# Turning three normalized chunks through VectorE and memory in place of TensorE transposes

## The chip, the cores and the metric

The kernel runs on one core of one Trainium2 chip. The metric is the device time of one execution in microseconds (us), the median of three runs. TensorE (PE in the profile) does the matrix products, VectorE (DVE) and ScalarE (ACT) read and write the accumulators in PSUM, GpSimd (POOL) works on SBUF alone, and SyncE (SP) issues nearly all transfers. Each engine takes its instructions strictly in the order in which the program wrote them.

## The reference

Four layers follow one another: attention A, feed-forward B, attention A, feed-forward B, each added to its input. There are 2048 rows of 448 values, 16 heads of 28, one key and value head shared by all, and a feed-forward of width 1792.

```python
q = (x @ wq) per head;  k = x @ wk;  v = x @ wv
p = softmax(q k^T * 28**-0.5);   A(x) = (p v) @ wo
B(x) = (silu(x @ w_gate) * (x @ w_up)) @ w_down
x = x + A(layernorm(x)); x = x + B(layernorm(x)); x = x + A(layernorm(x)); x = x + B(layernorm(x))
```

All of it is float32. The kernel keeps that precision by splitting each operand into a high part, rounded to the matrix format, and a low part, the rest; a product is then three matmuls: high by high, high by low, low by high.

## The kernel before, in words

The 2048 rows are handled as four chunks of 512 rows (chunk c is rows 512c to 512c+511), each chunk as four tiles of 128 rows on the 128 partitions. `xres` holds the running sum in SBUF.

Before a layer multiplies, a chunk is normalized (`norm_steps`, lines 210 to 233: statistics on VectorE, the scale on GpSimd, the normalized tile `xn` by VectorE with 64 columns copied by GpSimd) and turned, so that features lie on partitions. `flip` (lines 241 to 262) does the turning with TensorE: four 128x128 transposes make one 128x512 PSUM bank, `flipped` then has the bank copied, rounded, into `xh`, and the rest, bank minus `xh`, put into `xl` by VectorE. There are four such banks to a chunk. 448 features are three and a half times 128, so in the fourth bank the upper 64 partitions hold the rest of the same features, with `xd` as a copy of their high part.

Attention (`scores`, lines 530 to 692) runs 16 iterations i, four heads of one chunk each, of 16 steps kt. In a step TensorE makes 128x2048 scores, ScalarE takes their exponential in two instructions (lines 573, 574) and TensorE multiplies two steps later by the values (line 604). At step 10 of iterations 4, 8 and 12 `between_steps` puts in the output product of the chunk that is done (line 551). Around it `post` collects a finished iteration's sums: small transfers `rs`, `rd`, `rb`, and one product and one split on GpSimd (lines 615 to 643). For the iteration after next, four transfers fetch `qraw` at step 4, GpSimd splits it at step 7 and a transfer adds the `rows` at step 9.

Feed-forward needs the chunks turned again. In the kernel before

- chunk 0 is normalized in iteration 5 and flipped in the output-product slots of iterations 8 and 12, two banks in each, through the single bank `one`;
- chunk 1 is normalized in iteration 13 and flipped at the head of `FeedForward.rest` (line 863), after the last output product;
- chunks 2 and 3 are normalized in `rest` and soon after, and flipped in the middle of the units that go before their first use (line 870, `mid`).

Feed-forward's work is units: `unit(gi, c, n)` (line 791) multiplies chunk c with one block of 128 features of gate and up in two halves (lines 801 to 814), with down-products of the unit before between and behind them. The two first units, of chunk 0, run inside `scores`, ahead of the last chunk's output product; the next in program order are the two of chunk 1, the two of chunk 2, the two of chunk 3. In every half the matmuls run through the four 128-row blocks of the turned chunk in order, the last of the half needing the upper rows of the fourth block. `accumulate` (line 731) adds a finished group to `xres`: two of four tiles through a `stage` buffer and GpSimd (line 743). The buffers of the turned chunks 1 to 3 (`xb`) lie in the memory that the attention's own buffers (`wp`) leave at its end.

A second version of the whole program (`full`) stands in a branch at the end that the profiled execution does not take.

The order on every engine is the order in which the code calls the instructions; nothing reorders it.

Of the kernel before, what the change touches and what calls it, by code (L numbers as in the profile page):

```python
# [8 lines left out]
F32 = mybir.dt.float32  # L9
# [6 lines left out]
P = 128  # L16
# [38 lines left out]
def forward(  # L55
# [154 lines left out]
    def norm_steps(c, pool=pers):  # L210

        got = {}
        cs = slice(4 * c, 4 * c + 4)

        def stat(t):
            nc.vector.bn_stats(stats[:, 4 * c + t, :], xres[:, 4 * c + t, :])
            nc.vector.bn_aggr(mv[:, 4 * c + t, :], stats[:, 4 * c + t, :])

        def scale():
            rstd = pers.tile([P, 4], F32, name="rstd", bufs=2)  # L220
            nc.gpsimd.tensor_scalar(rstd, mv[:, cs, 1], 1.0, EPS, ALU.mult, ALU.add)
            nc.gpsimd.tensor_tensor(rstd, rstd, halfn, ALU.pow)
            got["r"] = rstd

        def apply(t):
            if t == 0:
                got["x"] = pool.tile([P, 4, 512], F32, name="xn")
            o, i, r = got["x"][:, t, 0:D], xres[:, 4 * c + t, :], got["r"][:, t : t + 1]
            nc.vector.tensor_scalar(o, i, mv[:, 4 * c + t, 0:1], r, ALU.subtract, ALU.mult)  # L229
            nc.gpsimd.tensor_copy(got["x"][:, t, D:512], o[:, 384:D])  # L230

        fs = [lambda t=t: stat(t) for t in range(4)] + [scale]
        return fs + [lambda t=t: apply(t) for t in range(4)], got
# [7 lines left out]
    def flip(got, tiles, ks=range(4), place=None):  # L241

        for k in ks:
            pt = place if place is not None else bank(wide[-1])[1]
            for t in range(4):
                nc.tensor.transpose(pt[:, P * t : P * t + P], got["x"][:, t, P * k : P * k + P], ident)  # L246
            flipped(tiles, k, pt, nc.vector.tensor_copy if place is not None else nc.scalar.copy)

    def flipped(tiles, k, pt, copy):
        xh, xl, xd = tiles  # L250
        if k < 3:
            copy(xh[:, k, :], pt)
            nc.vector.tensor_tensor(xl[:, k, :], pt, xh[:, k, :], ALU.subtract)  # L253
            return
        if xd is None:
            copy(xh[:, k, :], pt)
            high = xh[64:128, k, :]
        else:
            copy(xh[0:64, k, :], pt[0:64, :])
            copy(xd[64:128, :], pt[64:128, :])  # L260
            high = xd[64:128, :]
        nc.vector.tensor_tensor(xh[64:128, k, :], pt[64:128, :], high, ALU.subtract)

    def product_T(po, a_h, a_l, tiles):

# [37 lines left out]
    class Attention:  # L303
# [226 lines left out]
        def scores(self, ff):  # L530
            next(switch)
            with tc.tile_pool(name=f"at{self.layer}", bufs=1) as wp:
# [44 lines left out]
                def between_steps(n):  # L577

                    i, kt = divmod(n, NT)
                    free, one = threes[(n + 1) % 2], banks[7]  # L580
                    if full:
                        self.lent = free[:, 0, :]
                        self.advance(KC)
                        if kt == 11 and i + 1 < len(GR):
                            self.places[i + 1](free[:, 1, :])
                    if not todo or kt != 10:
                        return
                    c = todo.pop()
                    ks = list({8: (0, 1), 12: (2, 3)}.get(i, ()))
                    adds = []  # L590
                    for t in (1, 2, 3):
                        adds.append(outproj(c, t, free[:, t - 1, :]))
                        if ks:
                            flip(got, X0, [ks.pop(0)], one)
                    for f in adds:
                        f()
                    outproj(c, 0, one)()
# [45 lines left out]
                    return rest  # L643

                X0 = xtile(xpool)
                fs, got = norm_steps(0)
                fs1, got1 = norm_steps(1)
                ff.norms[1] = got1
                ff.second = norm_steps(2)
                last = NT * len(GR)  # L650
                for n in range(last):
                    i, kt = divmod(n, NT)
                    if kt == 4 and 2 < i + 2 < len(GR):
                        self.stack(i + 2)
                    if kt == 7 and 2 < i + 2 < len(GR):
                        self.parts(i + 2)
                    if kt == 9 and 2 < i + 2 < len(GR) and not full:
                        self.rows(i + 2)
                    if i in (2, 3) and kt == 8:
                        load_wo(i - 2)  # L660
                    if n == NT and ff.nxt:
                        ff.nxt.below(nc.sync)
                    if kt == 8 and 10 < i <= 11 + FG:
                        ff.W[i - 11] = weights(i - 11)
                    step(n)
                    if not full:
                        between_steps(n)
                    if n > 1:
                        pv(n - 2)
                    if full:  # L670
                        between_steps(n)
                    if n in due:
                        due.pop(n)()
                    if i in (5, 13, 14) and kt > 5:
                        for f in {5: fs, 13: fs1, 14: ff.second[0][:5]}[i][kt - 6 : kt - 5]:
                            f()
                for n in (last - 2, last - 1):
                    pv(n)
                self.lent = None
# [16 lines left out]
    class FeedForward:  # L696
        def __init__(self, layer):
            self.layer, self.X, self.W, self.norms = layer, {}, {}, {}
            self.pend, self.soon, self.dn, self.flip, self.mid, self.left = [], [], {}, 0, {}, []
            self.nxt = Attention(1) if layer == 0 else None  # L700

        def down(self, fs, fc, d, hh, hl):

# [53 lines left out]
        def hand_over(self, c):  # L757

            a = self.nxt
            fs, got = norm_steps(c)  # L760
            for f in fs[:5]:
                f()
            a.pool = self.stage
            a.X[c] = xtile(xpool if c == 0 else self.xbp)

            def ready():
                for f in fs[5:]:
                    f()
                if c > 1:
                    a.norms[c] = got  # L770

            if c == NC - 1:
                a.plan[8, 0] = [ready]
                return
            self.soon.append([1, ready])
            if c < 2:
                self.mid[len(groups) - 1, c + 2, 0] = [lambda ks=ks: flip(got, a.X[c], ks) for ks in ((0, 1), (2, 3))]
                self.soon.append([2, lambda: [a.project() for _ in range(2 - c)]])

        def turned(self, c, ks=range(4)):  # L780
            if c not in self.X:
# [74 lines left out]
        def rest(self, xb):  # L856
            self.stage = xb.enter_context(tc.tile_pool(name=f"stage{self.layer}", bufs=2))
            self.xbp = xb.enter_context(tc.tile_pool(name=f"xb{self.layer + 1}", bufs=3))
            xd = xb.enter_context(tc.tile_pool(name=f"xd{self.layer}", bufs=1))
            self.xd = [xd.tile([P, 512], F32R, name=f"xd{c}") for c in range(NC)]  # L860
            dma(self.xd[0][64:128, :], self.X[0][0][0:64, 3, :])
            self.X[0] = (*self.X[0][:2], self.xd[0])
            self.turned(1)
            fs2, self.norms[2] = self.second
            fs3, self.norms[3] = norm_steps(3)
            for f in fs2[5:] + fs3[:5]:
                f()
            self.soon.append([1, lambda: [f() for f in fs3[5:]]])
            for c in (2, 3):
                self.mid[0, c - 1, 1] = [lambda c=c, ks=ks: self.turned(c, ks) for ks in ((0, 1), (2, 3))]  # L870
            for gi, fs in enumerate(groups):
                if self.layer == 1 and fine is not None and gi in (2, 3):
                    self.verdict(gi == 3)
                    if gi == 3:
                        tc.mark_branch_hint_location("again", engines=(ET.Activation, ET.DVE, ET.Pool, ET.SP, ET.PE))
                for c in range(NC):
                    for n in range(len(fs)):
                        if gi or c:
                            self.unit(gi, c, n)
# [90 lines left out]
```

## Time and profile before

| what | us |
|---|---|
| median of three runs | 2043.53 (2042.91 to 2044.38) |
| span of the profiled execution | 2041.5 |
| what lies outside the span, median less span | 2.0 |
| PE busy / ACT busy / POOL busy / DVE busy in it | 2018.5 / 1311.0 / 536.7 / 460.0 |
| attention scores, first and second | about 75 to 596 and 1083 to 1604 |
| feed-forward, first and second | about 596 to 1000 and 1604 to 2041 |

The page gives no separate time for the profiled execution but its span; the 2.0 us between it and the median are taken as what lies around the span. A row of a timeline gives start and duration in us, engine, source line, operation, the tile written and the tiles read, the count of instructions merged in the row, and in brackets how long the engine sat idle before it and what ended that. A row of windows gives, for a stretch, each engine's busy time and count, the granted clock of TensorE (PEclk, 1.00 is full), the share of the transfer engines and GB/s.

### The profile page before, as it was taken

What the parts mean: (1) busy time and instruction counts of PE and PEld (TensorE: products, weight loads), DVE (VectorE), ACT (ScalarE), POOL (GpSimd) and SP (SyncE); (2) the same over time, 40 slices, a digit from 0 to 9 for tenths busy, and PEclk for the clock granted to TensorE, in tenths of its full rate; (3) what the DMA queues carried; (4) which work ended last, traced back from release to release, by engine and by line L of the source; (5) the groups of instructions that cost most, each with busy time, mean ns of one, the idle gap of its engine ahead of it and who ended that gap; (6) DMA issues with size and microseconds to landing.
All of it is one profiled execution on the core that took longest, in us unless ns stands there. A gap on an engine that the chain in (4) does not pass through costs nothing.

```text
span 2041.5 us, 43675 instructions
## 1 busy us (share of the span) xinstructions
PE 2018.5 (99%) x18627; PEld 1275.7 (62%) x18627; DVE 460.0 (23%) x890; ACT 1311.0 (64%) x2152; POOL 536.7 (26%) x601
## 2 busy tenths in 40 slices
PE   8999999999999999999999999999999999999998
PEld 7533434334348999999883334343343689988887
DVE  6300101001104323222451001010011242232322
ACT  3699898997973333333348998979979533333332
POOL 4313121021302333333341221111222122333320
PEclk9999999999999999999999999999999999999999
DMA  4201000011100111100031110100110000111102
GB/s 146 66 22 28 21 12 22 12 37 27 32 12 19 31 31 31 31 16 26 21 93 34 30 30 12 22 12 22 27 45 13 25 17 20 31 31 31 31 1 74
DMA packets 76512, 63.44 MB, mean 31 GB/s; under 512 B 22904, under 2 KB 63224, under 8 KB 76312
## 3 DMA queue, kind: packets, MB, share of 16 engines
q1 hardware_dynamic: 74580, 58.93, 10.4%
q8 instruction: 147, 2.41, 0.5%
q10 hardware_dynamic: 1732, 1.66, 0.3%
q14 instruction: 53, 0.43, 0.1%
HBM read 47.72 MB, written 12.32 MB: 29 GB/s over the span
## 4 chain that ended last, share of the span: by engine, by line
PE 50%; ACT 46%; DVE 1%; issue 1%; DMA 1%; POOL 0%; ACTq 0%; SPq 0%; DVEq 0%; POOLq 0%
PE bank L292 39%; ACT pt L574 31%; ACT pt L573 15%; PE bank L272 4%; PE three L551 2%; PE bank L551 2%; PE bank L246 1%; PE bank L604 1%; DMA wr<-in_A_wk_dram 1%; PE three L567 0%; DVE xl L253 0%; DMA kt<-stage 0%; DVE xn L229 0%; PE bank L398 0%; DVE vt L505 0%
## 5 line engine op out<-in xcount | busy, mean ns | idle before, releaser
L574 ACT ACTIVATE pt<-three 128x1536 f32<-128x1536 f32 x512 | 741.2, 1448 | 0.0
L604 PE MATMUL bank<-pt,vsb 128*32 128x512 f32 x4096 | 547.0, 606 | 0.5 <-ACT pt L574 0.5
L567 PEld LDWEIGHTS three<-qstack,keys 32*128 32x128 f32 x4608 | 252.9, 183 | 449.7 <-ACT pt L573 393.2
L567 PE MATMUL three<-qstack,keys 32*128 32x512 f32 x4608 | 498.5, 426 | 2.3 <-DVE vt L505 1.1
L567 PE MATMUL bank<-qstack,keys 32*128 32x512 f32 x1536 | 493.5, 426 | 2.9 <-ACT pt L573 2.9
L292 PE MATMUL bank<-xh,wgh 64*128 64x512 f32 x1728 | 447.6, 390 | 0.4
L292 PE MATMUL bank<-xh,wgl 64*128 64x512 f32 x1404 | 368.2, 390 | 0.0
L573 ACT ACTIVATE pt<-bank 128x512 f32<-128x512 f32 x512 | 305.8, 597 | 74.3 <-PE bank L567 68.1
L292 PE MATMUL bank<-xl,wgh 64*128 64x512 f32 x1296 | 335.1, 390 | 0.0
L292 PE MATMUL bank<-wdh,h 64*128 64x448 f32 x1792 | 331.2, 364 | 1.2 <-ACT h L827 0.8
L292 PEld LDWEIGHTS bank<-xh,wgh 64*128 64x128 f32 x1728 | 262.9, 184 | 19.1 <-DVE xl L253 1.5
L743 POOL TENSOR_TENSOR xres<-stage,xres 128x448 f32<-128x448 f32 x108 | 127.4, 1199 | 497.9 <-ACT stage L742 497.9
L638 POOL TENSOR_TENSOR o<-o 128x512 f32<-128x512 f32 x32 | 41.1, 1285 | 821.5 <-DMA o<-rd 748.5
L292 PEld LDWEIGHTS bank<-wdh,h 64*128 64x128 f32 x1792 | 242.5, 184 | 15.2 <-issue 2.7
L567 PEld LDWEIGHTS bank<-qstack,keys 32*128 32x128 f32 x1536 | 244.3, 183 | 4.5 <-ACT pt L573 4.3
L299 ACT COPY seen<-bank 128x1 f32<-128x1 f32 x664 | 81.7, 163 | 247.3 <-PE bank L292 244.4
L292 PEld LDWEIGHTS bank<-xh,wgl 64*128 64x128 f32 x1404 | 216.6, 184 | 13.8
L292 PE MATMUL bank<-wdl,h 64*128 64x448 f32 x896 | 217.7, 366 | 0.0
L825 ACT ACTIVATE sg<-bank 128x512 f32<-128x512 f32 x112 | 67.3, 601 | 220.0 <-PE bank L292 214.9
L292 PEld LDWEIGHTS bank<-xl,wgh 64*128 64x128 f32 x1296 | 196.3, 184 | 10.5
L604 PEld LDWEIGHTS bank<-pt,vsb 128*32 128x32 f32 x4096 | 80.9, 108 | 190.0 <-issue 175.2
L826 DVE TENSOR_TENSOR sg<-bank,sg 128x512 f32<-128x512 f32 x112 | 77.4, 691 | 500.0 <-ACT sg L825 491.1
(115 smaller groups left out, 1736.6 us busy)
## 6 DMA issues: line engine op xcount, KB each, us to landing
o<-rd SPq DMA_DIRECT2D x32, 256.0 KB
qd<-stage SPq DMA_DIRECT2D x32, 224.0 KB
qraw<-qd SPq DMA_DIRECT2D x128, 56.0 KB
wdr<-in_B_w_down_dram SPq DMA_DIRECT2D x28, 224.0 KB
wr<-in_B_w_gate_dram SPq DMA_DIRECT2D x28, 192.0 KB
wr<-in_B_w_up_dram SPq DMA_DIRECT2D x28, 192.0 KB
out_dram<-xres SPq DMA_DIRECT2D x15, 224.0 KB
wrk<-kt SPq DMA_DIRECT2D x8, 256.0 KB
```

Source lines behind the costliest of these rows:

```text
L272: nc.tensor.matmul(po, a, b, start=(i == 0), stop=(i == len(seq) - 1))
L292: nc.tensor.matmul(po, a, b, start=start, stop=stop, skip_group_check=True)
L299: nc.scalar.copy(seen[:, i : i + 1], po[:, 0:1])
L551: nc.tensor.matmul(po[:, 0:D], a[:, g, ts_], b[:, g, :], start=(g + z == 0), stop=(g == NG - 1 and z == 2))
L567: nc.tensor.matmul(three[:, j, :] if j < 3 else one, k[js, kp, ks], q[js, part, :], start=(z == 0), stop=(z == 2), tile_position=(32 * j, 0),)
L573: nc.scalar.activation(pt1, one, AF.Exp, scale=SCALE)
L574: nc.scalar.activation(pt, three, AF.Exp, scale=SCALE)
L604: nc.tensor.matmul(accs[i][32 * j : 32 * j + 32, :], vsb[:, kt, :], pts[n][j], start=(kt == 0), stop=(kt == NT - 1), skip_group_check=True,)
L638: nc.gpsimd.tensor_tensor(rb, oraw, rb, ALU.mult)
L743: nc.gpsimd.tensor_tensor(r, s, r, ALU.add)
L825: nc.scalar.activation(sg, pg[0], AF.Silu)
L826: nc.vector.tensor_tensor(sg, pg[1], sg, ALU.mult)
```

## The change

Chunks 0, 1 and 2 ahead of each feed-forward are no longer turned by TensorE. In attention's iterations 5, 9 and 13 a chunk is normalized, one call at each of steps 6 to 14. At the next four steps (step 15 and steps 0 to 2 of the following iteration) `turn_tile` has VectorE transpose a 128x512 tile in blocks of 32x32 into a new buffer `tb`, and SP issues four transfers that carry the blocks, in pieces of 128 bytes, to their places in a 512x512 tensor in memory, which then holds the turned chunk: 16 transfers to a chunk.

Chunk 0 is read back in iteration 7 by one 1 MB transfer and split by GpSimd (`halved`) at its steps 5, 8, 11 and 14. Chunk 1 is read back into `xn` in iteration 15, and `rest` begins with its split by GpSimd (`parts`): for each of three blocks a rounding copy and a subtraction, for the fourth two 64-partition copies and a subtraction, nine operations. Then SP reads chunk 2 into the same `xn` (`fetch(2)`), and GpSimd splits it likewise. Chunk 3 is flipped by TensorE as before.

```diff
+    def turn_tile(got, tb, raw, t):
+        nc.vector.transpose(tb[:, t, :], got["x"][:, t, :])
+        to = raw.rearrange("(b d) (t g w) -> t g d b w", d=32, g=4, w=32)
+        for g in range(4):
+            nc.sync.dma_start(to[t, g], tb[32 * g : 32 * g + 32, t, :].rearrange("d (b w) -> d b w", w=32))
+
+    def halved(tiles, r, ks=range(4)):
+        xh, xl, xd = tiles
+        for k in ks:
+            if k < 3:
+                split(xh[:, k, :], xl[:, k, :], r[:, k, :])
+        if 3 not in ks:
+            return
+        if xd is None:
+            nc.gpsimd.tensor_copy(xh[:, 3, :], r[:, 3, :])
+            high = xh[64:128, 3, :]
+        else:
+            nc.gpsimd.tensor_copy(xh[0:64, 3, :], r[0:64, 3, :])
+            nc.gpsimd.tensor_copy(xd[64:128, :], r[64:128, 3, :])
+            high = xd[64:128, :]
+        nc.gpsimd.tensor_tensor(xh[64:128, 3, :], r[64:128, 3, :], high, ALU.subtract)
...
-                        if ks:
-                            flip(got, X0, [ks.pop(0)], one)
...
+                for c in range(NC - 1):
+                    fs, got = norm_steps(c)
+                    ff.raw[c] = dram.tile([512, 512], F32, name=f"xt{self.layer}_{c}")
+                    fs += turns(c, got)
+                    for n, f in enumerate(fs):
+                        aside[16 * (4 * c + 5) + 6 + n] = f
+                for n, f in enumerate(back()):
+                    aside[16 * 7 + 2 + 3 * n] = f
+                aside[16 * 15 + 2] = lambda: ff.fetch(1)
...
+        def fetch(self, c):
+            self.got[c] = pers.tile([P, 4, 512], F32, name="xn")
+            nc.sync.dma_start(self.got[c], self.raw[c].rearrange("(k p) n -> p k n", p=P))
+
+        def parts(self, c):
+            self.X[c] = xtile(self.xbp, self.xd[c])
+            halved(self.X[c], self.got.pop(c))
...
-            self.turned(1)
-            fs2, self.norms[2] = self.second
+            self.parts(1)
+            self.fetch(2)
+            self.parts(2)
             fs3, self.norms[3] = norm_steps(3)
-            for f in fs2[5:] + fs3[:5]:
+            for f in fs3[:5]:
                 f()
             self.soon.append([1, lambda: [f() for f in fs3[5:]]])
-            for c in (2, 3):
-                self.mid[0, c - 1, 1] = [lambda c=c, ks=ks: self.turned(c, ks) for ks in ((0, 1), (2, 3))]
+            self.mid[0, 2, 1] = [lambda ks=ks: self.turned(3, ks) for ks in ((0, 1), (2, 3))]
```

More of the change, by code (lines that the diff above doesn't have):

```diff
@@ L588, in between_steps @@
                     c = todo.pop()
-                    ks = list({8: (0, 1), 12: (2, 3)}.get(i, ()))
                     adds = []
@@ L645, in scores, with turns, one, back @@
                 X0 = xtile(xpool)
[L646 to L649, printed above, removed]
+                def turns(c, got):
+                    at_ = {}
+                    def one(t):
+                        if t == 0:
+                            at_["tb"] = wp.tile([P, 4, 512], F32, name="tb")
+                        turn_tile(got, at_["tb"], ff.raw[c], t)
+                    return [lambda t=t: one(t) for t in range(4)]
+                def back():
+                    at_ = {}
+                    def load():
+                        at_["r"] = wp.tile([P, 4, 512], F32, name="tb")
+                        nc.sync.dma_start(at_["r"], ff.raw[0].rearrange("(k p) n -> p k n", p=P))
+                    return [load] + [lambda k=k: halved(X0, at_["r"], [k]) for k in range(4)]
+                aside = {}
+                for c in range(NC - 1):
[7 more added lines that the diff above has]
+                aside[16 * 15 + 2] = lambda: ff.fetch(1)
                 last = NT * len(GR)
@@ L673, in scores @@
                         due.pop(n)()
-                    if i in (5, 13, 14) and kt > 5:
-                        for f in {5: fs, 13: fs1, 14: ff.second[0][:5]}[i][kt - 6 : kt - 5]:
-                            f()
+                    if n in aside:
+                        aside[n]()
                 for n in (last - 2, last - 1):
@@ L700, in __init__ @@
             self.nxt = Attention(1) if layer == 0 else None
+            self.raw, self.got = {}, {}
         def down(self, fs, fc, d, hh, hl):
```

## The prediction

> **What bounds the kernel now.** I read the page first: the busy line, the granted clock and the chain that ended last.
>
> ```profile
> PE 2018.5 (99%) x18627; PEld 1275.7 (62%) x18627; DVE 460.0 (23%) x890; ACT 1311.0 (64%) x2152; POOL 536.7 (26%) x601
> PEclk9999999999999999999999999999999999999999
> PE 50%; ACT 46%; DVE 1%; issue 1%; DMA 1%; POOL 0%; ACTq 0%; SPq 0%; DVEq 0%; POOLq 0%
> ```
>
> Half the chain is PE (feed-forward, projections, output products) and half ACT (the exponentials of attention); DVE, POOL and the transfers carry nearly none. So what DVE and SP are given is free as long as nobody waits for it, and the question is where PE or ACT waits for turned chunks. There are three such places, the same in both layers: the output-product slots of iterations 8 and 12, the head of feed-forward (chunk 1), and the middle of its second unit pair (chunk 2).
>
> Slots: the timeline of ACT at step 10 of iterations 4, 8 and 12 in layer 1 (the idle time stands in the bracket), two rows of plain steps for the step length, and the row of the list of waits that groups them.
>
> ```profile
> 228.85 0.60 ACT L573 ACTIVATE pt<-bank 128x512 f32<-128x512 f32 x1 [10.16 <-PE bank L567]
> 230.80 0.60 ACT L573 ACTIVATE pt<-bank 128x512 f32<-128x512 f32 x1
> 232.69 0.60 ACT L573 ACTIVATE pt<-bank 128x512 f32<-128x512 f32 x1
> ...
> 361.48 0.60 ACT L573 ACTIVATE pt<-bank 128x512 f32<-128x512 f32 x1 [11.04 <-PE bank L567]
> ...
> 494.46 0.60 ACT L573 ACTIVATE pt<-bank 128x512 f32<-128x512 f32 x1 [11.33 <-PE bank L567]
> ACT pt L573 <- PE bank L567: 68.1, 10, 11.3
> ```
>
> Iteration 4 has no flips, 8 and 12 have two banks each: they cost 0.88 and 1.17 us. The list has 68.1 us in ten waits, and twice (10.16 + 11.04 + 11.33) is 65.1, so layer 2 pays the same.
>
> Head of feed-forward: the chain between 615 and 665 us, and one row of the PE timeline there.
>
> ```profile
> 616.59 2.62 PE bank L551 x12
> 619.21 0.45 PE bank L246 x4
> ...
> 621.65 10.08 PE bank L292 x83
> 631.72 1.03 PE bank L246 x8
> ...
> 634.18 1.02 PE bank L246 x8
> 624.07 0.36 PE L292 MATMUL bank<-wdh,h 64*128 64x448 f32 x1
> ```
>
> The last output product ends at 619.21, chunk 1 is flipped, and the first half of its first unit is through at 624.07, where the first down-product starts. Chunk 2's flips sit at 631.72 and 634.18. What they really take shows in the spacing of ACT's silu, one to a unit:
>
> ```profile
> 628.01 0.60 ACT L825 ACTIVATE sg<-bank 128x512 f32<-128x512 f32 x1 [1.96 <-PE bank L292]
> 637.75 0.60 ACT L825 ACTIVATE sg<-bank 128x512 f32<-128x512 f32 x1 [1.29 <-PE bank L292]
> 645.49 0.60 ACT L825 ACTIVATE sg<-bank 128x512 f32<-128x512 f32 x1 [1.96 <-PE bank L292]
> 662.98 0.60 ACT L825 ACTIVATE sg<-bank 128x512 f32<-128x512 f32 x1 [1.96 <-PE bank L292]
> 670.28 0.60 ACT L825 ACTIVATE sg<-bank 128x512 f32<-128x512 f32 x1 [2.14 <-PE bank L292]
> ```
>
> A plain unit is 7.30 us (662.98 to 670.28). The unit with chunk 2's flips takes 9.74, the one after it 7.74: together 2.9 us over.
>
> **The change, part by part.** All sums are per layer, against the profiled execution (span 2041.5 us); the median of the runs shown is 2.0 us above that, and I carry the 2.0 as constant.
>
> 1. Slots of iterations 8 and 12: without flips they should take what iteration 4's takes: 0.88 + 1.17 = -2.05 us.
>
> 2. DVE's transposes and the transfers in attention. The nearest rows, of the groups by shape, of SP's timeline twice, and the rate line of the transfer view of 14 to 19 us, when those two large reads ran:
>
> ```profile
> L400 DVE STREAM_TRANSPOSE sg<-bank 128x512 f32<-128x512 f32 x8 | 5.7, 717 | 22.0 <-PE bank L398 21.9
> 110.11 2.50 SPq L620 DMA_DIRECT2D rs<-o  x4
> 11.58 2.87 SPq L887 DMA_DIRECT2D xres<-in_A_x_dram  x2
> GB/s 375 390 418 418 405 360 434 403 419 361 404 433 393 328 328 181 195 237 185 327 401 430 416 373 358 430 430 401 373 416 444 387 351 300 228 97 65 71 71 67
> ```
>
> Twelve transposes are 8.6 us on DVE, 23% busy over the span and unused in those steps. SP issues 16 transfers to a chunk, 0.63 us each by the small ones (2.50 for 4), 1.43 by the 896 KB ones (2.87 for 2): 10 to 23 us of SP, over four steps. Queued behind on SP: that iteration's sums (`rs`, `rd`, `rb`), then `qraw` of the iteration after next, which POOL must split, and its rows. It is issued at step 4 and first multiplied 28 steps later, 28 x 1.89 = 53 us, so even 23 us of delay stays covered; without the cover it would be ACT that stops. No row shows 128-byte pieces written to memory alone, so I bound this from 0 to the 23 us less the cover: 0. Chunk 0's split (9 us of POOL in iteration 7) is covered likewise. I take 0 for all of it.
>
> 3. Head of feed-forward, the main term. In the program's order POOL's first split instruction waits for the last L551 matmul, because the new `xh` lies in memory that the output product still reads. POOL's prices, copy and subtraction of the same 128x512 shape, with starts that show the gap between instructions:
>
> ```profile
> 611.10 1.29 POOL L638 TENSOR_TENSOR o<-o 128x512 f32<-128x512 f32 x1 [27.55 <-DMA o<-rd]
> 612.48 0.62 POOL L134 TENSOR_SCALAR onh<-o 128x512 fp32r<-128x512 f32 x1
> 613.18 1.28 POOL L135 TENSOR_TENSOR onl<-o,onh 128x512 fp32r<-128x512 f32 x1
> 628.17 1.01 POOL L222 TENSOR_TENSOR rstd<-rstd,halfn 128x4 f32<-128x4 f32 x1
> 630.50 2.35 POOL L743 TENSOR_TENSOR xres<-stage,xres 128x448 f32<-128x448 f32 x2 [1.32 <-ACT stage L742]
> ```
>
> Gap 0.08. Three blocks of 0.62 + 1.28 + two gaps = 6.18; the fourth, two half-width copies of the same length (0.70 each with gap) and a subtraction, 2.68. Together 8.86 us from about 619.3: done at 628.17. PE follows at POOL's pace; its last two pairs of matmuls (0.23 us apart, rows further down) come after, so the first down-product starts at 628.63, not 624.07: +4.55 us. Nothing covers it; PE has no other work in front. This already contains the gain of chunk 1's own flips.
>
> 4. Chunk 2. Its flips go: -2.05 (the two PE pieces, 1.03 + 1.02) to -2.9 (the spacing). I take the middle, -2.45, since the 0.44 in the unit behind may remain as a start-up wait. But is the tile there? The rows for that:
>
> ```profile
> 641.79 0.39 ACT L299 COPY seen<-bank 128x1 f32<-128x1 f32 x2 [2.06 <-PE bank L292]
> 605.86 0.58 SPq L631 DMA_DIRECT2D o<-rd  x1
> ```
>
>  SP may issue the read only when POOL has read chunk 1, at 628.17: 1.43 to issue, 1.05 MB at the 400 GB/s above 2.6 us more, and 0 to 3 us until it has landed (the 256 KB read at L631 took 5.2 in all, 605.86 to POOL's L638 at 611.10): 632 to 635. POOL's 8.86 then ends between 641 and 644. The first half of chunk 2's first unit needs its last piece at about 641.6 before (ACT's `seen` follows it at 641.79), so at 641.6 + 4.55 - 2.45 = 643.7 now, and later by whatever term 5 adds. I take 0, with 0 to 1 us kept for the range. Behind it POOL owes the scale for chunk 3 (0.20 + 1.01), then the sums of chunk 0 (2.35, which ACT's stage buffers wait for two units later): both are done by 648, the next user comes after 650.
>
> 5. TensorE's clock. The windows of the trace in which PE works in bursts (row: window, PE busy; the seventh figure is the clock), and the PE timeline at a change of clock:
>
> ```profile
> 71.68:75.10 3.42, 1.74 (x23) 1.26 (x24) 3.27 (x5) 1.19 (x2) 2.88 (x7) 1.00 0.33 112
> 75.10:78.51 3.41, 3.29 (x21) 1.32 (x20) 0.31 (x1) 3.02 (x4) 0.00 (x0) 0.50 0.16 32
> 78.51:81.93 3.42, 3.42 (x24) 1.04 (x20) 0.00 (x0) 1.83 (x3) 0.35 (x1) 0.50 0.27 78
> 1078.61:1082.03 3.42, 2.48 (x19) 1.05 (x17) 1.83 (x3) 1.03 (x2) 1.49 (x7) 1.00 0.59 170
> 1082.03:1085.44 3.41, 1.48 (x16) 0.71 (x16) 2.72 (x5) 2.52 (x4) 2.21 (x4) 1.00 0.03 10
> 1085.44:1088.86 3.42, 3.42 (x21) 1.02 (x21) 0.00 (x0) 3.04 (x3) 0.00 (x0) 0.50 0.23 58
> 20.07 0.59 PE L272 MATMUL bank<-xh,wl 128*128 128x512 f32 x1
> 20.50 0.40 PE L272 MATMUL bank<-xh,wh 128*128 128x512 f32 x1
> 20.73 0.39 PE L272 MATMUL bank<-xl,wh 128*128 128x512 f32 x1
> ```
>
> A stretch of 3.41 us with PE 43 to 51% busy (1.48, 1.74) is followed by half clock, for one or two such stretches, though PE is busy in them; one with 73% (2.48) is not. In the 8.9 us of term 3 PE gets three pairs of matmuls, some 0.5 + 0.7 us of busy time, per 2.06 us of POOL, and two pairs in the last 2.7 us: 4.0 of 8.9, 45%. At least one whole stretch falls in it, so I expect half clock from there until the first stretch that is busy throughout has ended: 3.41 to 6.83 us after POOL is done, 5.1 in the mean. At half clock a matmul follows in 0.43 us (20.07 to 20.50) and not 0.23 (20.50 to 20.73), so 0.465 of that time is lost: +1.6 to +3.2, I take +2.4.
>
> The Trainium skill ("TensorE: Matmul & The Clock Gate", Part 1) gives a free-running window of about 3.4 us, half clock after an idle one and full clock after a busy one; the windows agree on length and half. Its table names an idle window, which this stall is not; that reading is rival B.
>
> Sum: -2.05 + 4.55 - 2.45 + 2.4 = +2.45 us a layer, +4.9 for two: span 2046.4, time 2048.4 us.
>
> **Rivals.**
> A, faster: the split starts before the output product ends. POOL is free at 614.46 (613.18 + 1.28); were `xh`'s memory free then, it would be done at 623.4 and the first half at 623.9, 0.2 earlier than before, with no clock loss: -2.05 - 0.2 - 2.45 = -4.7 a layer, 2034.1. It decides (faster by over 0.2%) once POOL starts 2.1 us earlier than 619.3 with the clock kept, 4.5 us without. Against it: the wait named in term 3, on the very last matmul.
> B, no clock loss: the bursts count as activity. Then +0.05 a layer, with -2.9 for chunk 2 -0.4: 2042.7 to 2043.6, the same. For it: the longest gap in the bursts is about 2 us, less than a stretch; against it: 1.48 and 1.74 us were too little twice. By the skill's table read literally, with no idle window, the clock would stay.
> C, chunk 2 late too: if its read takes 11 us, not 4 to 7, POOL ends at 648, 1.9 us behind 643.7 + 2.4: 2 x (2.45 + 1.9) = +8.7, 2052.2. Against it: 400 GB/s at the start of the kernel; for it: the weights' transfers queue right behind it.
>
> **How the numbers follow.** Main case 60%, A 6%, B 24%, C 10%. The main case's own range, by its ends (clock 1.6 to 3.2, chunk 2 -2.9 to -2.05): 2 x (-2.05 + 4.55 - 2.9 + 1.6) = +2.4 to 2 x (-2.05 + 4.55 - 2.05 + 3.2) = +7.3, so 2045.9 to 2050.8. The range for 8 in 10 takes in B below and C above: 2042.7 to 2053. 0.2% (4.1 us) is about what a measurement of this kernel can tell from no change, so faster means below 2039.4 and slower above 2047.6. About a fifth of the main case lies below 2047.6. Slower: 0.48 + 0.10 = 0.58; same: 0.24 + 0.12 = 0.36; faster: 0.06.
>
> **What the profile after would show.** Right: ACT's wait at iterations 8 and 12 is 10.2 us; POOL's L134 at the head of feed-forward starts within 0.2 us of the last L551 matmul, and PE's first L292 matmuls there wait for POOL; the first down-product starts 9.4 us after the output product's end (4.86 before); the clock row reads 0.50 for some 7 to 10 us there and nowhere else anew; silu of chunk 2's units waits for PE alone; qstack's splits keep their place. Wrong: a clock of 1.00 throughout (term 5), L134 starting early (term 3), PE waiting for POOL at chunk 2 (term 4), or ACT waits in iterations 6, 7, 10 or 14 (term 2).

## The result, and the profile after

| | us |
|---|---|
| before, median of 15 executions | 2043.77 (2042.72 to 2045.51) |
| changed, median of 15 executions | 2047.69 (2046.01 to 2048.87) |
| ratio | 1.0018, 95% interval 1.0011 to 1.0024 |
| predicted | 2048.4 (2042.7 to 2053.0) |
| profiled execution of the changed kernel, time and span | 2048.7 and 2047.0 |

The change costs 3.9 us, 0.19%. The interval excludes no change, but by the 0.2% that the prediction took as its bound it is still "the same", 0.2 us short of "slower", to which the prediction had given 0.58. The forecast time is 0.7 us above the median.

The page of the changed kernel, engines, packets and chain:

```profile
PE 2016.9 (99%) x18531; PEld 1272.4 (62%) x18531; DVE 458.6 (22%) x882; ACT 1300.7 (64%) x2132; POOL 586.9 (29%) x653
DMA packets 130367, 76.01 MB, mean 37 GB/s; under 512 B 73688, under 2 KB 114008, under 8 KB 130168
PE 50%; ACT 46%; issue 1%; DMA 1%; DVE 1%; POOL 1%; ACTq 0%; SPq 0%; POOLq 0%; DVEq 0%
```

POOL has 50 us more to do than before (536.7), and the shares of the chain hardly move. POOL's 1% lies in two places of some 8.4 us, one at the head of each feed-forward; the page alone does not say where or what they cost.

The two slots: ACT's timeline of the changed kernel, at step 10 of iterations 8 and 12 of layer 1.

```profile
361.02 0.60 ACT L597 ACTIVATE pt<-bank 128x512 f32<-128x512 f32 x1 [10.10 <-PE bank L591]
493.00 0.60 ACT L597 ACTIVATE pt<-bank 128x512 f32<-128x512 f32 x1 [10.28 <-PE bank L591]
```

The waits were 11.04 and 11.33 us: 0.94 + 1.05 = 2.0 us are gone, as forecast.

The head of feed-forward: the chain of the changed kernel there, then from TensorE's timeline the first down-product.

```profile
615.36 2.64 PE bank L575 x12
...
618.22 0.63 POOL xh L134
...
625.39 1.27 POOL xh L286
626.66 0.04 issue
626.70 13.43 PE bank L316 x88
```

```profile
627.30 0.57 PE L316 MATMUL bank<-wdh,h 64*128 64x448 f32 x1
```

POOL begins 0.22 us after the last output product (615.36 + 2.64 = 618.00) and its split is the chain from there to 626.66. The first down-product follows the output product after 9.30 us, 4.86 before: +4.44.

Windows of 3.41 us of the changed kernel over this stretch (PE busy first, the granted clock after POOL's figure):

```profile
618.24:621.65 3.41, 1.58 (x8) 0.67 (x8) 3.20 (x9) 0.00 (x0) 3.24 (x4) 1.00 0.18 41
621.65:625.07 3.42, 2.58 (x10) 1.67 (x11) 0.00 (x0) 0.00 (x0) 3.28 (x5) 0.50 0.00 0
625.07:628.48 3.41, 2.49 (x13) 1.65 (x12) 0.00 (x0) 0.32 (x2) 1.50 (x2) 0.50 0.05 16
628.48:631.89 3.41, 3.41 (x20) 2.99 (x18) 0.00 (x0) 0.45 (x4) 0.00 (x0) 0.50 1.00 352
631.89:635.31 3.42, 3.42 (x32) 3.01 (x32) 1.22 (x2) 1.20 (x3) 2.84 (x4) 1.00 0.53 149
```

One window in which PE is busy for 1.58 of 3.41 us is followed by three at half clock, 10.24 us. POOL is done in the second of these three, so for 5.2 us (626.70 to 631.89) PE has all its operands and runs at half clock. The busy time in a half-clock window is inflated (its matmuls last longer), so 2.58 and 2.49 do not mean that PE worked more there.

The clock's share shows in silu, ACT's first step of each unit's end, here for chunk 1's two units and chunk 2's first, and in the arrival of chunk 2 (SP's read, POOL's first and last instruction on it):

```profile
633.36 0.60 ACT L883 ACTIVATE sg<-bank 128x512 f32<-128x512 f32 x1 [2.82 <-PE bank L316]
640.65 0.60 ACT L883 ACTIVATE sg<-bank 128x512 f32<-128x512 f32 x1 [1.99 <-PE bank L316]
647.94 0.60 ACT L883 ACTIVATE sg<-bank 128x512 f32<-128x512 f32 x1 [1.96 <-PE bank L316]
```

```profile
626.67 0.38 SPq L831 DMA_DIRECT2D xn<-xt  x1
```

```profile
632.31 0.62 POOL L134 TENSOR_SCALAR xh<-xn 128x512 fp32r<-128x512 f32 x1 [5.66 <-DMA xn<-xt]
...
639.97 1.29 POOL L286 TENSOR_TENSOR xh<-xn,xd 64x512 fp32r<-64x512 f32 x1
```

From the output product's end to chunk 1's first silu it was 628.01 - 619.21 = 8.80 us and is 633.36 - 618.00 = 15.36: +6.56, of which +4.44 is POOL's pace and 2.1 the clock. The next two spacings are 7.29 + 7.29 where they were 9.74 + 7.74 with chunk 2's flips: -2.90, and chunk 2 waits for nobody. So layer 1 comes to -2.0 + 6.56 - 2.9 = +1.7, and in layer 2 the same three places come to +1.5 (-2.0 + 6.25 - 2.7). Together that is +3.2, of the +3.9 measured. The two profiled executions lie 5.5 us apart. Of the 2.3 us between, 1.0 lies in the first iteration of the second attention (32.67 us from its first exponential to the next iteration's, 31.66 before), where half clock lasted 3.41 us in the profiled execution before (1085.44 to 1088.86) and 6.83 in the one after; where the other 1.3 us lie was not followed up.

```profile
1085.87:1089.28 3.41, 3.25 (x21) 1.85 (x21) 1.28 (x2) 3.05 (x3) 0.89 (x1) 0.50 0.12 22
1089.28:1092.69 3.41, 3.41 (x25) 1.04 (x20) 0.00 (x0) 2.04 (x3) 0.00 (x0) 0.50 0.19 74
```

This varies from one execution to the next, in the kernel before too (the run named turning_only below is that kernel once more, and its profiled execution has 6.83 us there). It makes a microsecond of scatter between single profiles that has nothing to do with the change.

### The profile page after: what moved, and what is told of

Read it like the earlier page. It is cut to its first block, busy times and chain, and to the rows that moved or that the text cites. A ratio compares the mean times of both kernels' runs of the same rounds, so it can differ in the third digit from the quotient of the medians.

```text
span 2047.0 us, 43637 instructions
## 1 busy us (share of the span) xinstructions
PE 2016.9 (99%) x18531; PEld 1272.4 (62%) x18531; DVE 458.6 (22%) x882; ACT 1300.7 (64%) x2132; POOL 586.9 (29%) x653
## 4 chain that ended last, share of the span: by engine, by line
PE 50%; ACT 46%; issue 1%; DMA 1%; DVE 1%; POOL 1%; ACTq 0%; SPq 0%; POOLq 0%; DVEq 0%
PE bank L316 39%; ACT pt L598 31%; ACT pt L597 15%; PE bank L296 5%; PE three L575 2%; PE bank L575 2%; PE bank L246 1%; PE bank L625 1%; DMA wr<-in_A_wk_dram 1%; PE three L591 0%; POOL xl L135 0%; DMA kt<-stage 0%; PE bank L591 0%; PE bank L422 0%; DVE xn L229 0%
## 5 line engine op out<-in xcount | busy, mean ns | idle before, releaser
L316 PE MATMUL bank<-xh,wgh 64*128 64x512 f32 x1728 | 442.9, 392 | 3.7 <-POOL xh L286 1.8
```

The costliest lines, as they stand in the source:

```text
L316: nc.tensor.matmul(po, a, b, start=start, stop=stop, skip_group_check=True)
```

## The experiments

Theory: the slots and chunk 2's flips are gains of 2.0 and 2.9 us a layer; chunk 1's split loses them, some two thirds by GpSimd's pace and one third by the clock that falls in the stall. Rivals: the half clock costs nothing because TensorE waits anyway; the turning costs something in attention; the stall is the wait for memory, not GpSimd's pace. All times stand beside the kernel before on the same chip, 2043.1 to 2043.8; where they are compared with the changed kernel, that is its 2047.69, measured beside 2043.77.

**The clock, first try.** While TensorE waits for GpSimd in chunk 1's first half, it gets matmuls that nobody needs.

```diff
...
+            count = {0: 3, 1: 4, 3: 1, 4: 4, 6: 1, 7: 4, 9: 8}
...
+            def fill(i):
+                for _ in range(count.get(i, 0)):
+                    nc.tensor.matmul(spare, self.W[0][0][:, 0, 0, :], self.X[0][0][:, 0, :], start=True, stop=True, ...)
```

> The changed kernel, and nothing of it moved, but while TensorE waits for GpSimd in the first half of chunk 1's first unit it is given matmuls of chunk 0's tile into a bank that nobody reads (25 of them: 3 ahead of the first pair, 4 ahead of each low-part pair, 1 ahead of the next block, 8 ahead of the last block). They are surplus work and change no result. Theory (the clock falls because TensorE works only in bursts there, and that costs what the head lost beyond GpSimd's pace): the head of feed-forward lost 6.66 and 6.26 us in the spacing of silu, of which GpSimd's pace explains 9.30 - 4.86 = 4.44; the rest is 2.2 + 1.8 = 4.0 us. The clock row stays at 1.00 there, first down-product still 9.3 us behind the output product's end, time 4.0 us under the changed kernel: about 2043.7, level with the kernel before. Rival (the half clock costs nothing, TensorE waits for GpSimd anyway and the 4.0 us are from elsewhere): 2047.7 or, by the surplus matmuls, up to 1 us more.

2046.51 us, 1.0013 [1.0003, 1.0022]: 1.2 under the changed kernel, between theory and rival. The clock stayed at 1.00 in the trace, but TensorE, not GpSimd, was now the last: the first down-product came 11.2 us after the output product. Too much fill, so it settles nothing on the price. (One of the eleven executions took 6671 us; its cause is open. The ratio leaves it out; without it the median is 2046.39.)

**The clock, lighter.** 17 pairs in the unit's own form of 64 rows in place of 25 full matmuls.

```diff
...
+            count = {0: 2, 1: 3, 4: 3, 7: 3, 9: 6}
...
+                    for z in range(2):
+                        rs = slice(64 * z, 64 * z + 64)
+                        nc.tensor.matmul(spare[z], self.W[0][0][rs, 0, 0, :], self.X[0][0][rs, 0, :], ...)
```

> As the first filled kernel, but with less surplus work and in the form of the unit's own matmuls (pairs of 64 rows: 2 pairs at the start, 3 ahead of each low-part pair, 6 ahead of the last block; results unused). There the fills kept the clock at 1.00 but themselves became the pace: the first down-product came 11.2 us after the output product's end, not 9.3, and the time fell by 1.2 us only. Theory (the half clock costs 2.2 + 1.8 us at the two heads): clock 1.00 through the head, first down-product 9.3 to 9.6 us after the output product, so 1.5 to 2.2 a layer less than the changed kernel: 2043.5 to 2044.8. Rival (clock at 1.00, but the head loses its 6.3 to 6.7 us all the same): 2046.5 to 2047.7.

2045.45 us, 1.0006 [0.9997, 1.0015]. Its windows over the stall, the chain's last output product, the first down-product and two silu steps:

```profile
618.24:621.65 3.41, 3.29 (x22) 2.15 (x24) 3.25 (x9) 0.00 (x0) 3.22 (x4) 1.00 0.18 41
621.65:625.07 3.42, 3.09 (x24) 1.71 (x24) 0.00 (x0) 0.00 (x0) 3.28 (x5) 1.00 0.02 5
625.07:628.48 3.41, 3.17 (x29) 2.50 (x27) 0.00 (x0) 0.48 (x3) 1.58 (x2) 1.00 0.00 0
```

```profile
615.40 2.64 PE bank L577 x12
```

```profile
627.12 0.36 PE L318 MATMUL bank<-wdh,h 64*128 64x448 f32 x1
```

```profile
631.07 0.60 ACT L886 ACTIVATE sg<-bank 128x512 f32<-128x512 f32 x1 [1.96 <-PE bank L318]
638.83 0.60 ACT L886 ACTIVATE sg<-bank 128x512 f32<-128x512 f32 x1 [2.08 <-PE bank L318]
```

POOL's pace is untouched: the down-product comes 627.12 - 618.04 = 9.1 us after the output product, 9.3 without the fill. But the silu is there after 13.03 us, not 15.36: with the clock kept, 2.3 us come back, and 2.0 in layer 2. That is the price of the half clock, shown by itself.

The kernel as a whole gained 2.2 and not 4.3, so the time is 0.65 us above the range that the theory gave, and 1.05 under the rival's: a part of the gain is given back at once. The next spacing is 7.76 in both layers, where the changed kernel has 7.29 and 7.51, and the one behind it is 7.30 in layer 1 but 8.19 in layer 2. What TensorE waits for there, one row from each of these two places:

```profile
632.46 0.49 PE L318 MATMUL bank<-xh,wgh 64*128 64x512 f32 x1 [0.17 <-DVE sg L887]
```

```profile
1650.74 0.49 PE L318 MATMUL bank<-xh,wgh 64*128 64x512 f32 x1 [0.64 <-POOL xh L286]
```

The 7.76 is the fill's own cost: chunk 1's second unit waits for VectorE's last read of the first unit's sums. The changed kernel has no such wait; the fill takes two banks of the same four in turn, which is the likely reason. Only the 8.19 is chunk 2's tile, which is late in layer 2, where its read took 7.05 us. In layer 1 the tile, which had been in time behind a late head, is still in time.

**GpSimd's pace.** Chunk 1 is split by ScalarE (copies) and VectorE (subtractions), all else as changed.

```diff
-    def halved(tiles, r, ks=range(4)):
+    def halved(tiles, r, ks=range(4), quick=False):
+        if quick:
+            for k in ks:
+                flipped(tiles, k, r[:, k, :], nc.scalar.copy)
+            return
...
-            halved(self.X[c], self.got.pop(c))
+            halved(self.X[c], self.got.pop(c), quick=c == 1)
```

> The changed kernel, but chunk 1 (not 0, not 2) is split from the copy in SBUF by ScalarE (rounding copies) and VectorE (subtractions) instead of GpSimd. Theory (GpSimd's pace is the stall, 1.94 us a block): a block then takes about 0.7 us (VectorE's subtraction of this shape 0.69), the first down-product follows the output product's end by 0.6 + 4 x 0.7 + 0.4 = 3.8 us, not 9.3 and not the 4.86 of the flips; no window at half clock; with -2.05 for the slots and -2.9 for chunk 2 that is -2.05 - 1.05 - 2.9 = -6.0 a layer against the kernel before: about 2031.8. Rival 1 (the stall is the wait for the memory that the output product reads, and what follows it, whichever engine splits): no better than the changed kernel's head, 2043 to 2048. Rival 2 (the stall is cured, but chunk 2's tile, read earlier, still comes late): 2034 to 2038.

2034.33 us, 0.9952 [0.9938, 0.9966]: 13.4 under the changed kernel by one replacement of nine instructions. ScalarE's first copies, VectorE's subtractions, the first down-product, SP's read of chunk 2, POOL's first instruction on it, and silu of chunk 1's second and chunk 2's first unit:

```profile
617.35 1.66 ACT L252 CAST xh<-xn 128x512 fp32r<-128x512 f32 x3 [3.22 <-PE bank L579]
```

```profile
618.00 1.89 DVE L253 TENSOR_TENSOR xl<-xn,xh 128x512 fp32r<-128x512 f32 x3
```

```profile
621.29 0.36 PE L320 MATMUL bank<-wdh,h 64*128 64x448 f32 x1
```

```profile
620.93 0.38 SPq L835 DMA_DIRECT2D xn<-xt  x1
```

```profile
628.12 0.62 POOL L134 TENSOR_SCALAR xh<-xn 128x512 fp32r<-128x512 f32 x1 [14.64 <-ACT stage L794]
```

```profile
632.54 0.60 ACT L887 ACTIVATE sg<-bank 128x512 f32<-128x512 f32 x1 [2.15 <-PE bank L320]
641.41 0.60 ACT L887 ACTIVATE sg<-bank 128x512 f32<-128x512 f32 x1 [1.96 <-PE bank L320]
```

The head takes 3.96 us (621.29 after an output product that ends at 617.33) and the clock stays at 1.00. The split still begins only when the output product has ended (617.35), so the wait for that memory is there as before and does not cost the 4.4 us: rival 1 falls. Rival 2 holds in part: the read took 7.2 us and chunk 2 came late, 8.87 between the silu steps where 7.29 is a plain unit, 1.6 us in layer 1 (0.2 in layer 2). That is most of the 2.5 us missing to the 2031.8 expected.

**Chunk 0 alone.**

```diff
-                for c in range(NC - 1):
+                for c in range(1):
...
-                aside[16 * 15 + 2] = lambda: ff.fetch(1)
+                fs1, got1 = norm_steps(1)
+                ff.norms[1] = got1
+                ff.second = norm_steps(2)
...
-            self.parts(1)
-            self.fetch(2)
-            self.parts(2)
+            self.turned(1)
+            fs2, self.norms[2] = self.second
```

> Only chunk 0 goes the new way (turned by VectorE in iteration 5, 16 transfers, read back and split by GpSimd in iteration 7); chunks 1 and 2 are normalized and flipped where the kernel before does it. Theory (the flips in iterations 8 and 12 cost 0.88 + 1.17 us each layer, all else of chunk 0's new way is covered): -2.05 a layer, -4.1 in all, about 2039.7. Rival (transfers, VectorE or GpSimd in iterations 5 to 7 take some of it back): 2041 to 2044.

2041.60 us, 0.9989 [0.9980, 0.9998], 2.2 us where 4.1 were expected: between theory and rival. In the trace the slots give all that they should; ACT's waits in its two slots of layer 1, against 11.04 and 11.33:

```profile
361.26 0.60 ACT L597 ACTIVATE pt<-bank 128x512 f32<-128x512 f32 x1 [10.10 <-PE bank L591]
493.15 0.60 ACT L597 ACTIVATE pt<-bank 128x512 f32<-128x512 f32 x1 [10.08 <-PE bank L591]
```

So 0.94 + 1.25 in layer 1, and 4.0 over both layers. The interval reaches 4.1, and this profiled execution, too, had 6.83 us of half clock at the start of the second attention, which takes 1.0 us of the gain in it. What chunk 0's new way costs in iterations 5 to 7, where it is normalized, turned, read back and split, can be read from the trace: ACT's first exponential of iterations 5 and 8 in layer 1, before and in this kernel.

```profile
238.38 0.60 ACT L573 ACTIVATE pt<-bank 128x512 f32<-128x512 f32 x1
329.48 0.60 ACT L573 ACTIVATE pt<-bank 128x512 f32<-128x512 f32 x1
```

```profile
239.01 0.60 ACT L597 ACTIVATE pt<-bank 128x512 f32<-128x512 f32 x1
330.18 0.60 ACT L597 ACTIVATE pt<-bank 128x512 f32<-128x512 f32 x1
```

The three iterations take 91.17 us and took 91.10, and 91.16 in layer 2 of both kernels: the new way costs 0.1 us at most. The next run puts the turning alone to the test.

**Turning beside the kernel before.** The first attempt did not contain what its expectation says: the steps were prepared and never called, so it was the kernel before once more.

> The kernel before with nothing taken away, and the turning of the changed kernel added beside it: in iterations 5, 9 and 12 of each layer VectorE's four transposes and SyncE's sixteen transfers of 128-byte pieces to memory, at the same steps as in the changed kernel; nobody reads the result. Theory (term 2 of the prediction: all of it is covered): 2043.75, within 0.7. Rival (taking the flips of chunk 0 away alone brought 2.15 us and not 4.1, because the turning costs part of the gain, some 1 us per chunk and layer): 2047 to 2050.

It gave 2043.75 beside 2043.63, and is of use only as a measure of repetition: 0.1 us. Then with the calls in place:

```diff
+                    if n in aside:
+                        aside[n]()
```

> The kernel before with nothing taken away, and the turning of the changed kernel added beside it, this time really called (in the run named turning_only the calls were prepared but never made, so that run was the kernel before once more): at the ends of iterations 5, 9 and 12 of each layer VectorE's four transposes and SyncE's sixteen transfers of 128-byte pieces to memory, 96 transfers in all; nobody reads the result. Theory (term 2 of the prediction: all of it is covered): 2043.6, within 0.7. Rival (taking the flips of chunk 0 away alone brought 2.15 us and not 4.1, because the turning costs part of the gain, some 1 us per chunk and layer): 2047 to 2050.

2043.76 us beside 2043.48, 1.0000 [0.9991, 1.0009], although the packets went from 76512 to 127201. SP's timeline with the sixteen transfers of one chunk and the sums behind them:

```profile
264.18 4.13 SPq L269 DMA_DIRECT2D xt<-tb  x8
272.98 2.47 SPq L627 DMA_DIRECT2D rs<-o  x4
275.55 4.48 SPq L269 DMA_DIRECT2D xt<-tb  x8
...
283.79 1.77 SPq L387 DMA_DIRECT2D qraw<-qd  x4
```

0.52 to 0.56 us each, 8.6 us of SP a chunk. What stands behind is late (the fetch of `qraw` starts at 283.79 and did at 279.06), and nobody waits for it. The rival falls. Two things differ from the changed kernel: all three turnings carry chunk 0's tile, and the last sits in iteration 12, not 13.

**Chunk 2's part.** First chunk 2 back on TensorE, 0 and 1 the new way:

```diff
-            self.fetch(2)
-            self.parts(2)
+            fs2, self.norms[2] = self.second
...
-            self.mid[0, 2, 1] = [lambda ks=ks: self.turned(3, ks) for ks in ((0, 1), (2, 3))]
+            for c in (2, 3):
+                self.mid[0, c - 1, 1] = [lambda c=c, ks=ks: self.turned(c, ks) for ks in ((0, 1), (2, 3))]
```

> Chunks 0 and 1 go the new way, chunk 2 is normalized and flipped in the middle of chunk 1's second unit as in the kernel before. Theory (the third part of the change alone is worth 2.9 us a layer): the changed kernel's time plus 5.8, about 2053.5. Rival (behind a head that is late anyway, chunk 2's flips cost less, or GpSimd's freed time helps the rest): 2048 to 2051.

2052.82 us, 1.0047 [1.0033, 1.0060]: 5.1 above the changed kernel, 2.6 a layer where 2.9 were expected, with the same 10.24 us of half clock at each head. Then the reverse, only chunk 1 back on TensorE:

```diff
-                for c in range(NC - 1):
+                for c in (0, 2):
...
-            self.parts(1)
+            self.turned(1)
             self.fetch(2)
```

> Chunks 0 and 2 go the new way, chunk 1 is flipped by TensorE at the head of feed-forward as in the kernel before (it is normalized in iteration 14, after chunk 2 has been turned). Theory (the whole loss is chunk 1's split at the head, its pace and the clock; the two other parts are gains): -2.05 for the slots, head as before, -2.9 for chunk 2, whose split ends at about 636 and is needed at 639: -4.95 a layer, -9.9 in all, about 2033.9. Rival (chunk 2's tile was in time only because the head was long): the unit of chunk 2 waits for GpSimd, 2036 to 2040.

2034.52 us, 0.9953 [0.9939, 0.9966]: 9.2 under the kernel before (9.9 were expected), 13.2 under the changed one. Chunk 2's spacings are 7.29 and 7.29 in both layers. Its read is issued as soon as the flips have freed `xn` (618.74), and its split is over at 633.66, with time to spare. So two of the three parts gain, and chunk 1's alone turns the gain into a loss.

**A better kernel.** To the split by ScalarE and VectorE two things were added: chunk 2 is read into the place where chunk 3's tile will be written, so that the read need not wait for chunk 1, and GpSimd takes chunk 1's fourth block.

```diff
+            if c == 2:
+                for n in (1, 2, 3):
+                    self.X[n] = xtile(self.xbp, self.xd[n])
+                self.got[c] = self.X[3][0].bitcast(F32)
...
-            self.X[c] = xtile(self.xbp, self.xd[c])
...
-            self.parts(1)
             self.fetch(2)
+            self.parts(1)
...
-            for k in ks:
+            for k in range(3):
                 flipped(tiles, k, r[:, k, :], nc.scalar.copy)
-            return
+            ks = [3]
```

> The kernel in which ScalarE and VectorE split chunk 1, changed in two places: GpSimd takes chunk 1's fourth block beside them, and chunk 2 is read into the place where chunk 3's turned tile will lie, so that its read no longer waits until chunk 1 has been split. Theory (chunk 2 was late by 1.57 us in the first layer because its read was issued at 620.9 and took 7.2 us; the first down-product came at 621.29 because VectorE's last subtraction ended at 620.9): chunk 2 is in time, the first down-product comes about 0.7 earlier in each layer: 2034.3 - 1.6 - 1.4 = 2031.3. Rival (the fourth block is not the last wait and the read competes with the weights however early it is): 2033.5 to 2034.5.

2034.75 us, 0.9956 [0.9942, 0.9970]: no better than without. Chunk 2 was in time (7.29 and 7.29), but the head got longer, 5.15 us and not 3.96 (1.2 us more, where the next expectation says 0.9). VectorE's subtractions and GpSimd's last one in this kernel:

```profile
617.86 3.40 DVE L253 TENSOR_TENSOR xl<-xn,xh 128x512 fp32r<-128x512 f32 x3
```

```profile
619.11 1.60 POOL L290 TENSOR_TENSOR xh<-xn,xd 64x512 fp32r<-64x512 f32 x1
```

The same three subtractions took 1.89 us above. Taking the help away again, and nothing else:

```diff
-            for k in range(3):
+            for k in ks:
                 flipped(tiles, k, r[:, k, :], nc.scalar.copy)
-            ks = [3]
+            return
```

> The kernel with chunk 2's early read, but all four blocks of chunk 1 split by ScalarE and VectorE, none by GpSimd; nothing else differs. Where GpSimd took the fourth block beside them, VectorE's three subtractions took 3.40 us together (1.89 without GpSimd beside them) and GpSimd's own last one 1.60 (1.28), and the first down-product came 0.9 us later than without its help. Theory (VectorE and GpSimd slow one another when both read and write SBUF, so the help was none): VectorE's three subtractions back at 1.9 us, head 0.8 us under the kernel before in each layer, chunk 2 in time: 2034.75 - 2 x 0.95 = 2032.9. Rival (the early read of chunk 2 slows VectorE, not GpSimd): VectorE stays at 3.4 us, 2034.7.

```profile
619.00 1.90 DVE L253 TENSOR_TENSOR xl<-xn,xh 128x512 fp32r<-128x512 f32 x3
```

2032.39 us, 0.9946 [0.9933, 0.9960], with the head back at 3.96 us (622.29 after 618.33) and chunk 2 in time: theory and not rival, and the lowest median of all, 10.7 us under the kernel before beside it. Beside their own kernels before that is 14.6 us (10.7 + 3.9) under the changed kernel. What the early read alone is worth is not settled: by the ratios 1.2 us against the kernel without it, and the two intervals overlap. This kernel keeps the whole change but the engine of nine instructions and one read's place.

## Why the prediction was right, and where its sizes were off

All in us a layer, measured in layer 1.

| step | forecast | measured | by |
|---|---|---|---|
| 1, slots of iterations 8 and 12 | -2.05 | -2.0 | ACT's waits; the same in the kernel with chunk 0 alone |
| 2, turning and transfers in attention | 0 | 0.1 | turning beside the kernel before, +0.3 in all, within 1.8; iterations 5 to 7 of the kernel with chunk 0 alone |
| 3, GpSimd's pace at the head | +4.55 | +4.44 | first down-product 9.30 after the output product, 4.86 before |
| 4, chunk 2 | -2.45 | -2.9 | spacings of silu; 2.6 by the run with chunk 2 flipped |
| 5, half clock behind the stall | +2.4 | +2.1 | what is left of +6.56; 2.3 by the lighter fill, of which 0.2 stand in term 3's tail |

The mechanism was right, and each size was within half a microsecond. The sum came out at +1.7 and not +2.45 a layer, mainly because term 4 took its middle (-2.45) where the spacing (-2.9) was the better row: the 0.44 in the unit behind was the flips' doing, not a start-up wait. With -2.9 the sum would have been +2.0 a layer, 2047.5 us; the other 0.3 is mainly term 5. So the change itself was forecast 1.0 us too large (+4.9 against +3.9). That the time is only 0.7 us off is chance: the kernel before measured 0.2 us more here than in the three runs that the forecast started from. The 2.0 us that it took for what lies outside the span is 1.7 in the profiled execution after (2048.7 less 2047.0). Term 1 rested on iteration 4's slot as the model for the others; the slots now all take that.

Term 3's duration was 0.4 us too long (GpSimd's gap between dependent instructions is smaller than the 0.08 taken; 8.44 from first to last, not 8.86) while its start lay 0.1 later than taken and its tail, at half clock, was 0.2 longer: they nearly cancel.

Rival B, no clock loss, falls by the windows and by the lighter fill: bursts that made PE 46% busy in a window did not keep the clock. The Trainium skill ("TensorE: Matmul & The Clock Gate", Part 1) gives half clock after an idle window of about 3.4 us. The trace agrees on the length (10.24 us is three windows), but its window was not idle: 1.58 of 3.41 us in bursts were too little, while 3.09 were enough in the filled kernel.

Rival C, chunk 2 late, did not come true, but the tile was in time only because the head was late. In the changed kernel POOL was done with it at 641.26 (639.97 + 1.29), 2.5 us before TensorE came to its last block:

```profile
643.74 0.40 PE L316 MATMUL bank<-xh,wgh 64*128 64x512 f32 x2
```

Two kernels shortened the head and left the read behind chunk 1's split. With ScalarE and VectorE chunk 2 came late by 1.6 us in layer 1 and 0.2 in layer 2, with the lighter fill not at all in layer 1 and by 0.9 in layer 2. Term 4's "tile in time" was therefore right by the cover of terms 3 and 5, which the prediction gave only partly (643.7, "later by whatever term 5 adds"). The read took 5.6 us from issue to POOL's start here, 7.2 in another kernel, and not the 11 that rival C asked for.

Rival A, a split ahead of the output product's end, falls by the trace: POOL starts 0.22 us after that end. What a tile in other memory, free earlier, would bring was not tried.

## What to carry to other kernels

Moving work off a bounding engine pays only where the new engine's pace is hidden: the same split that costs nothing in the middle of attention (chunk 0) or behind two units (chunk 2) costs 6.6 us at a stage's head, where the bounding engine has nothing else to do. Here it paid to give that one piece to a faster pair of engines that was free. Price a stall of the matmul engine with the clock: here a stall that was 4.4 us longer than before brought 2.1 more at half clock after its end. And a tile that is in time behind a stall is to be checked again once the stall is mended, since its cover goes with it.

## What the runs showed of the hardware that was not expected

GpSimd beside VectorE slowed both when each split from SBUF: three VectorE subtractions of 128x512 took 3.40 us with GpSimd at work beside them and 1.90 without, in two kernels that differ in nothing else, and GpSimd's subtraction took 1.60 and not 1.29. VectorE's third ended at 621.26, 0.55 us after GpSimd's (620.71), where one alone takes 0.69: as if it had waited for GpSimd to finish. The Trainium skill ("SBUF — State Buffer", SBUF: two separate sides) states that a VectorE operation with two SBUF inputs and a GpSimd operation that reads SBUF exclude one another for a whole instruction; the trace agrees with such a loss, and ScalarE's copies beside VectorE showed none (1.89).

Half clock lasted until a window had been busy throughout: in the changed kernel the window from 625.07, which begins within the stall and ends 1.8 us after it, did not release the clock; the next, busy for all of its 3.41 us, did. The twelve traces of this case have forty such returns to full clock, and the last window at half clock was busy throughout in all of them. Windows ahead of it that were busy for up to 3.39 us did not release the clock (nor did two that were full; the next one did). The other way, within the program (a trace's start and end left aside) the clock fell after windows with up to 2.14 us busy and stayed after others with 2.10 us or more, so here the bound lies near 2.1 of 3.41 us.

Writes to memory in pieces of 128 bytes, 50,000 more packets, cost nothing that can be measured here (+0.3 us, within 1.8), where nobody waits for them.
